# Two hybrid layers on one core: constant products in TensorE's first gaps, the large loads on one queue, eight tiles of key exponents, a new order

## The chip, the core and the metric

The kernel runs on one core of a Trainium2 chip. The core has five engines with an instruction queue each: TensorE (PE in the profile; its weight loads are PEld), VectorE (DVE), ScalarE (ACT), GpSimd (POOL) and SyncE (SP). TensorE writes its products to PSUM, eight banks here (`pb`), from which VectorE and ScalarE take them. Transfers are issued from the queues of SP and ScalarE and run on 16 DMA engines. The engines wait for one another by semaphores. The metric is device time in microseconds (us) of the core.

## The reference

For x of 2048 rows and 512 columns in bfloat16, the same two layers run twice:

```python
x = x + A(layernorm(x))     # linear attention, 32 heads of 16
x = x + B(layernorm(x))     # gated unit of width 1376
# A:
q, k, v = split(x @ wqkv)
phi(u)  = concat(softmax(u @ w_phi), softmax(-(u @ w_phi)))   # over 16
kv, z   = phi(k)^T v, sum over rows of phi(k)
o       = (phi(q) kv) / (phi(q) z + 1e-6)
A       = o @ wo
# B:
gate = x @ W_gate;  gate = gate * (gate > 0);  B = (gate * (x @ W_up)) @ W_down
```

The sums kv and z run over all 2048 rows, so no row can be attended before the keys of all rows are done.

## The kernel before

The 2048 rows are 16 tiles of 128, in five slabs of 2, 4, 4, 4 and 2 tiles (`SLABS`). All of x stays in SBUF (`x_sb`), as do the weights. At the start `fold` multiplies w_phi into the key and query weights: the weights are transposed (the key quarters on TensorE, the query quarters by transposing loads), multiplied with a block-diagonal matrix BD made of w_phi, and stored as `Wkp` and `Wqp`.

For each layer, `layernorm` takes statistics (L813, L838), a logarithm and an exponential for the standard deviation (L840, L842), applies them (L855 on ScalarE, L858 on VectorE or POOL), and turns the tile round, on TensorE or by a transposing load of SP's queue (L863). `keys` then makes, tile by tile, products with `Wkp` and `wv` (L682), two exponentials (L915, `expk`), their sums over 16 (L921, `Zk`), reciprocals (L924 on VectorE, L927 and L928 on ScalarE), a copy of the values (`vsb`), and the two value products with the reciprocals (L935, `vhat`, on VectorE or POOL). Of these, TensorE makes small products of 32 by 34 (L947) that are added up in `kvsum` (L957). `expk` and `vhat` have five buffers, used in turn. After the last tile `sums` builds the matrices of the sums; per slab `queries` makes the exponentials of the queries (L1016, `expq`), and `attend` the sums (L1031 or L1044), the softmax's divisor, its spreading to all rows (L1153 with products, or L1089 and L1093 by way of memory into `abT`), the numerators (L1105), their copies (`oT`, two buffers by slab), the product with `wo` and the residual. `glu` makes gate and up (L1227, L1229) and the product with W_down.

The order of the work is not that of the code. Each operation is recorded with a cost, and `Program.schedule` places them one after the other by start and by the turn numbers of the table `TURNS`; the table `ENG` names the engine of each movable operation. The order that comes out is fixed for every engine's queue: an engine that waits for one operation holds all behind it. TensorE's shape of array changes between plain products, small products, strips and numerators (`mode`).

Loads before: ScalarE issues x tiles 2 and 3, tile 0, and tiles 4 to 7; SP issues tile 1, a key quarter, w_phi, three key quarters, x tiles 8 to 11, wv, two transposing query loads, x tiles 12 to 15, and the rest.

The program's lines are these; the planner's function `schedule` and the build.

## Time and profile before

| what | before |
|---|---|
| time, median of 3 runs | 387.96 us (387.41 to 388.64) |
| profiled execution: time, span | 387.48 us, 385.7 us |
| TensorE busy | 370.9 us, 96% of the span |
| VectorE, ScalarE, POOL busy | 272.9, 200.6, 57.5 us |
| mean granted clock of TensorE | 0.991 |
| first key product starts | 12.90 us |
| VectorE ends layer 0's last value product | 57.6 us |
| first product of the gated unit | 76.89 us |
| TensorE's last product ends | 382.2 us |

The span runs from the first to the last instruction. A share of busy time is a mean over stages with different limits, so the stretches between the marks of the table are read one by one. A line such as `L1105 ... x32` is a group of 32 instructions of line 1105. A time after "idle" or "waited for" is time in which an engine had nothing it could do, with what ended it. Idle time costs only where the engine sets the pace. A matmul's duration holds its latency; products in a row start closer together than they last.

### The profile page before, as it was taken

Reading aid. Unit: us, or ns where it says so; the run is one execution under the profiler, and the core shown is the slowest. Engines: PE = TensorE matmul, PEld = TensorE weight load, DVE = VectorE, ACT = ScalarE, POOL = GpSimd, SP = SyncE. Lnnn points to the kernel's source line nnn. Section 1 sums busy time; section 2 is a strip of 40 time slices with the busy share of each in tenths; the row PEclk is TensorE's granted clock in tenths of the full one; section 3 lists DMA queues with packets and bytes.
Section 4 is the critical chain, followed back from the end, with each engine's and each line's share of the span. In section 5 each row is a group of like instructions: output and inputs, shape, how many; then the busy total and the mean of one; then the engine's idle time right before and its main releaser. Section 6 shows DMA issues by size and latency. Waiting matters only on the chain.

```text
span 385.7 us, 9001 instructions
## 1 busy us (share of the span) xinstructions
PE 370.9 (96%) x3713; PEld 197.6 (51%) x3767; DVE 272.9 (71%) x562; ACT 200.6 (52%) x447; POOL 57.5 (15%) x57
## 2 busy tenths in 40 slices
PE   5899998999999999999999999999999999999996
PEld 2544554484444444544466555475444454444574
DVE  6999998889554895574697897689954566453343
ACT  3899989853452524163246789983344224232111
POOL 2055550020310000000132461002002011000000
PEclk9799999999999999999999999999999999999999
DMA  8992301055351222021002010123524131221011
GB/s 245 271 347 38 66 3 51 14 160 88 111 97 44 57 41 56 10 59 29 0 9 56 3 30 4 58 61 110 131 62 135 45 86 36 59 43 41 2 34 55
DMA packets 56969, 27.44 MB, mean 71 GB/s; under 512 B 39168, under 2 KB 55264, under 8 KB 56928
## 3 DMA queue, kind: packets, MB, share of 16 engines
q1 hardware_dynamic: 55840, 25.88, 26.8%
q10 hardware_dynamic: 1088, 0.98, 0.8%
q8 instruction: 29, 0.48, 0.5%
q14 instruction: 12, 0.10, 0.1%
HBM read 14.73 MB, written 4.00 MB: 49 GB/s over the span
## 4 chain that ended last, share of the span: by engine, by line
PE 77%; ACT 10%; DVE 7%; issue 2%; DMA 2%; POOL 1%; ACTq 0%; DVEq 0%
PE pb L682 74%; ACT expq L1016 3%; DVE Zk L921 2%; DMA x_sb<-in_A_x_dram 2%; ACT expk L915 2%; DVE vhat L935 2%; POOL vhat L935 1%; PE pb L947 1%; PE pb L1105 1%; ACT vsb L789 1%; ACT ytile L855 1%; DVE expq L1171 1%; ACT oT L789 1%; ACT abT L789 1%; ACT yA L789 1%
## 5 line engine op out<-in xcount | busy, mean ns | idle before, releaser
L682 PE MATMUL pb<-Wd,hT 128*128 128x512 bf16 (+2 forms) x352 | 93.0, 372 | 0.8 <-issue 0.3
L682 PE MATMUL pb<-yG,Wu 128*128 128x512 bf16 (+1 forms) x396 | 93.3, 336 | 0.3 <-issue 0.2
L682 PE MATMUL pb<-yG,Wg 128*128 128x512 bf16 (+1 forms) x393 | 91.4, 336 | 0.4
L1227 ACT ACTIVATE gate_sb<-pb 128x512 bf16<-128x512 f32 x80 | 46.7, 596 | 75.8 <-PE pb L682 57.7
L1229 DVE TENSOR_TENSOR hT<-gate_sb,pb 128x512 bf16<-128x512 bf16 x80 | 53.4, 682 | 44.2 <-PE pb L682 25.2
L935 POOL TENSOR_TENSOR vhat<-vsb,rZk 128x544 bf16<-128x544 bf16 x38 | 41.1, 1103 | 133.5 <-DVE vhat L935 85.7
L1175 DVE TENSOR_TENSOR x_sb<-x_sb,pb 128x512 bf16<-128x512 bf16 x59 | 39.3, 681 | 30.4 <-PE pb L682 30.1
L682 PEld LDWEIGHTS pb<-yG,Wu 128*128 128x128 bf16 x400 | 38.9, 98 | 32.5 <-ACT gate_sb L1227 0.4
L682 PEld LDWEIGHTS pb<-yG,Wg 128*128 128x128 bf16 x400 | 38.7, 98 | 30.0 <-DVE hT L1229 0.5
L682 PEld LDWEIGHTS pb<-Wd,hT 128*128 128x128 bf16 (+1 forms) x363 | 35.1, 98 | 35.9 <-issue 1.0
L915 ACT ACTIVATE expk<-pb 128x512 bf16<-128x512 f32 x64 | 34.8, 616 | 17.0 <-PE pb L682 15.7
L813 DVE BATCH_NORM_STATS2 stats<-x_sb 128x6 f32<-128x512 bf16 x60 | 39.9, 682 | 2.8 <-DMA x_sb<-in_A_x_dram 2.4
L921 DVE TENSOR_REDUCE Zk<-expk 128x64 f32<-128x1024 bf16 x32 | 37.9, 1204 | 0.4 <-ACT expk L915 0.2
L682 PE MATMUL pb<-wv,yA 128*128 128x512 bf16 x123 | 37.1, 381 | 1.0 <-issue 0.5
L682 PE MATMUL pb<-Wkp,yA 128*128 128x512 bf16 x119 | 36.7, 385 | 0.9 <-issue 0.6
L1016 ACT ACTIVATE expq<-pb 128x512 bf16<-128x512 f32 x64 | 34.8, 638 | 1.5 <-PE pb L682 1.4
L682 PE MATMUL pb<-wo_sb,oT 128*128 128x512 bf16 x122 | 33.4, 379 | 0.4 <-ACT oT L789 0.2
L682 PE MATMUL pb<-yA,Wqp 128*128 128x512 bf16 (+1 forms) x148 | 31.3, 334 | 1.4 <-issue 1.0
L1138 POOL TENSOR_TENSOR expq<-expq,abT 128x1024 bf16<-128x1024 bf16 (+1 forms) x8 | 14.0, 1761 | 123.4 <-PE pb L682 58.6
L1195 ACT ACTIVATE gate_sb<-pb 128x192 bf16<-128x192 f32 x16 | 5.3, 333 | 47.2 <-PE pb L682 47.2
L855 ACT ACTIVATE ytile<-x_sb,nmr,rstd 128x512 bf16<-128x512 bf16 x31 | 24.4, 825 | 2.8 <-DVE nmr L847 2.7
L682 PEld LDWEIGHTS pb<-yA,Wqp 128*128 128x128 bf16 x160 | 14.3, 98 | 12.0 <-issue 1.0
(97 smaller groups left out, 337.4 us busy)
## 6 DMA issues: line engine op xcount, KB each, us to landing
abT<-spread SPq DMA_DIRECT2D x32, 128.0 KB
out_dram<-x_sb SPq DMA_DIRECT2D x15, 128.0 KB, 1.8
Wu<-in_B_W_up_dram SPq DMA_DIRECT2D x1, 1280.0 KB
Wg<-in_B_W_gate_dram SPq DMA_DIRECT2D x1, 1280.0 KB
Wd<-in_B_W_down_dram SPq DMA_DIRECT2D x1, 1280.0 KB, 14.9
sums_scr<-abT SPq DMA_DIRECT2D x5, 256.0 KB, 2.5
Zs<-sums_scr SPq DMA_DIRECT2D x5, 256.0 KB, 2.9
x_sb<-in_A_x_dram SPq DMA_DIRECT2D x2, 512.0 KB, 6.8
```

The source lines that it names most:

```text
L682: op("pe", lambda e: e.matmul(view(ps), lhsT, rhs, start=start, stop=stop), reads=reads, writes=[ps], occ=max(25.0, 0.4167 * n + 2.6), lat ...
L789: op("act", lambda e: e.activation(dst(), src(), ACT.Copy), reads=[ps] + reads, writes=writes, occ=115 + 0.714 * n, lat=240 + 0.714 * n, n ...
L813: op("dve", lambda e: e.bn_stats(stats[:, t, :], src()), reads=[res], writes=[R("st", t)], occ=580, lat=680, name=f"bn{t}")
L855: op("act", (lambda t, yb: lambda e: e.activation(ytile[:, yb, :], x_sb[:, t, :], ACT.Identity, bias=nmr[:, t, :], scale=rstd[:, t, :]))(t ...
L915: op("act", (lambda i, s, pk: lambda e: e.activation(expk[:, i, s, :], full(pk), ACT.Exp, scale=1.0 - 2.0 * s))(i, s, pk), reads=[pk], wri ...
L921: op("dve", (lambda i, zb: lambda e: e.tensor_reduce(Zk[:, zb, :], expk[:, i, :, :].rearrange("p s (h f) -> p (s h) f", f=16), AX.X, ALU.a ...
L935: op(eng, (lambda i, s, vb, rz: lambda e: e.tensor_tensor(vhat[:, i, s, :, :], vsb[:, vb, :, :], rZk[:, rz, s * 32:(s + 1) * 32].unsqueeze ...
L1016: op("act", (lambda c0, s, ps: lambda e: e.activation(eqv(st)[:, c0:c0 + per, s, :], ps.f32()[:, 0:per * n].rearrange("p (c n) -> p c n", ...
L1138: op(eng, lambda e: e.tensor_tensor(part, part, abT[:, c].rearrange("p (s n) -> p s n", s=2)[:, :, 0:n], ALU.mult), reads=Re + [R("abT", c ...
L1175: op("dve", lambda e: e.tensor_tensor(x_sb[:, t, :], x_sb[:, t, :], full(ps), ALU.add), reads=[R("x", t), ps], writes=[R("x", t)], occ=597 ...
L1227: op("act", (lambda gb, pg, k: lambda e: e.activation(gate_sb[:, gb, 0:k], pg.f32()[:, 0:k], ACT.Relu))(gb, pg, k), reads=[pg], writes=[R( ...
L1229: op("dve", (lambda gb, hb, pu, k: lambda e: e.tensor_tensor(hT[:, hb, 0:k], gate_sb[:, gb, 0:k], pu.f32()[:, 0:k], ALU.mult))(gb, hb, pu, k),
```

## The change

Four things change together.

First, `filler` adds 18 products of a constant matrix (128x256) into PSUM banks that nobody reads: eight with constants on both sides, and ten with the first quarter of `Wkp` as the moving side, so that they come after it. Of the ten, three stand in the order after slab 0's second norm.

Second, the loads: ScalarE's queue issues x tile 0 and two key quarters. SP's issues tile 1, w_phi, tiles 2 and 3, tiles 4 to 7, two key quarters, wv, tiles 8 to 11, the four transposing query loads, tiles 12 to 15, and then the rest. The planner's costs of loads change with it (delays, a bandwidth of 345 instead of 360, a limit on what a queue holds).

Third, `expk` and `vhat` have eight buffers instead of five. Three of the exponents lie in `abT`, three of the value tiles in `oT`, which are otherwise used in the attention. So that they are free for layer 1's keys, the attention of layer 0's slabs 3 and 4 is recorded ahead of layer 1's second slab.

Fourth, `TURNS` and `ENG` are new: the engines of many copies, applies and products change, among them BD from POOL to VectorE and three applies from VectorE or ScalarE to POOL. The last tile's down product is cut at column 384 instead of 256.

```diff
-LASTCUT = ((0, 256), (256, 512))
+LASTCUT=((0,384),(384,512)); FILL=(8,10); LOADLATE=(100,150)
...
-    DMA_BW = 360.0
+    DMA_BW = 345.0
+    RING = 5500.0
...
-                free[o.eng] = s + o.occ
+                free[o.eng] = max(s + o.occ, qfree - self.RING)
...
-        NY, NE, NV, NG, NH = 8, 5, 4, 3, 18
+        NY, NE, NOWN, NV, NG, NH = 8, 8, 5, 4, 3, 18
...
-        expk = sb("expk", [NE, 2, 512])
-        vhat = sb("vhat", [NE, 2, 32, 17])
+        expk_own = sb("expk", [NOWN, 2, 512])
+        vhat_own = sb("vhat", [NOWN, 2, 32, 17])
...
+        oT_flat = oT[:].rearrange("p g c n -> p (g c n)")
+
+        def expk(i):
+            return expk_own[:, i] if i < NOWN else abT[:, i - NOWN, :].rearrange("p (s n) -> p s n", s=2)
+
+        def vhat(i):
+            return vhat_own[:, i] if i < NOWN else oT_flat[:, 1088 * (i - NOWN):1088 * (i - NOWN) + 1088].rearrange("p (s h e) -> p s h e", s=2, e=17)
...
+        def filler(k, reads, src):
+            for i in range(FILL[k]):
+                ps = bank(f"fill{k}{i}")
+                op("pe", (lambda ps: lambda e: e.matmul(ps.f32()[:, 0:256], ones[:, 0:128], src, start=True, stop=True))(ps),
+                   reads=R_ones + reads, writes=[ps], occ=109, lat=275, name="fill")
+
+        filler(0, [], ones[:, 0:256])
...
+        def attended_to(L, st):
+            if (L, st) not in attended:
+                attended.add((L, st))
+                prog.tag = f"q{L}{st}"
+                queries(st, buf[st])
+                attend(L, st)
...
         fold("k", Wknat, Wkp)
+        filler(1, [R("W", "k", 0)], Wkp[:, 0, 0:256])
...
+                    if st == 1:
+                        attended_to(0, 3)
+                        attended_to(0, 4)
                     into_a(1, st)
```

## The prediction

> **What bounds the kernel now.** I read the page's busy shares first, then busy time by stretch, then the chain of work that ended last, then who waited for whom, and last TensorE's own timeline.

> ```profile
> PE 370.9 (96%) x3713; PEld 197.6 (51%) x3767; DVE 272.9 (71%) x562; ACT 200.6 (52%) x447; POOL 57.5 (15%) x57
> ```

> TensorE is busy for all but 14.8 of 385.7 us, so no change that leaves its products alone can win much more than what it idles, waits in small pieces, or runs slowly. Where that is, the windows tell (busy of PE, PEld, DVE, ACT, POOL; then clock, DMA share, GB/s):

> ```profile
> 0.00:8.88 8.88, 4.83 (x23) 2.28 (x24) 5.05 (x20) 3.49 (x6) 2.42 (x11) 0.96 0.78 232
> 8.88:57.60 48.72, 46.19 (x843) 25.03 (x851) 48.13 (x94) 45.09 (x106) 21.58 (x20) 0.94 0.57 150
> 57.60:76.90 19.30, 17.69 (x347) 8.99 (x354) 16.27 (x43) 17.33 (x43) 0.00 (x0) 1.00 0.12 32
> 76.90:211.00 134.10, 133.04 (x869) 70.37 (x881) 94.79 (x197) 55.13 (x116) 12.91 (x9) 1.00 0.26 59
> 211.00:272.00 61.00, 59.69 (x983) 34.17 (x1008) 49.77 (x98) 46.48 (x109) 15.10 (x13) 1.00 0.17 48
> ```

> From 8.88 to 57.60 (keys of layer 0) VectorE is busy for 48.13 of 48.72: it sets the pace. From 76.90 TensorE does. Between them (queries, first attention) TensorE and ScalarE are both some 90% busy. The chain agrees; these are pieces of it (start, length, what):

> ```profile
> 1.82 7.04 DMA x_sb<-in_A_x_dram
> ...
> 42.13 2.34 DVE Zk L921 x2
> ...
> 55.07 2.55 DVE vhat L935 x4
> ```

> The loads begin it; at 57.6 VectorE ends the last value tile of layer 0. Two waits lie in the start:

> ```profile
> POOL hT L777 <- DMA wphi<-in_A_w_phi_dram: 4.6, 1, 4.6
> ...
> DVE stats L813 <- DMA x_sb<-in_A_x_dram: 2.4, 1, 2.4
> ```

> And there the granted clock (the number before DMA share) is half:

> ```profile
> 4.86:8.17 3.31, 0.78 (x9) 0.43 (x8) 1.62 (x5) 1.58 (x4) 1.04 (x1) 1.00 1.02 303
> 8.17:15.00 6.83, 5.78 (x36) 3.80 (x38) 5.97 (x20) 4.82 (x12) 0.00 (x0) 0.50 1.23 291
> ```

> Last, what small product groups cost TensorE (start, length):

> ```profile
> 28.32 1.03 PE L682 MATMUL pb<-wv,yA 128*128 128x512 bf16 x4 [0.16 <-POOL vhat L935]
> 29.28 0.68 PE L947 MATMUL pb<-vhat,expk 128*32 128x34 bf16 x64
> 30.12 0.92 PE L682 MATMUL pb<-yA,Wqp 128*128 128x512 bf16 x4 [0.16 <-issue]
> ```

> **The change, part by part.** The sum is made against the profiled execution, 387.48 us, of which 385.7 is span; the median of the three runs is 0.48 above it.

> *Stage 1, to VectorE's last value tile (57.6).* VectorE's work there is 53.18 us (5.05 and 48.13). The new order lists give it two value copies more (0.60 start to start), three 128x512 copies yA<-pb more (0.33), and the block-diagonal product, which leaves POOL; they take away a copy of Wkp and one of Wqp (0.60 each), a reciprocal (0.46) and a value product (0.63). The trace has the block-diagonal product on POOL alone (1.04); on VectorE I bound it by 0.40 (128x512 tensor-scalar) and 0.74 (128x544 tensor-tensor), and take 0.65. Sum: 1.20+0.99+0.65-0.60-0.60-0.46-0.63 = +0.55, so 53.73. Its idle was 0.98 at the start, 0.39 in the constants, 2.40 for the x load and 0.59 after. The 2.40 should go: the four-tile x load moves from third of the ScalarE queue, behind 384 KB, to fourth of SP's, behind 400 KB, with 384 KB instead of SP's megabyte beside it; the 1.3 MB of both queues up to its end take 5.6 us at the first stretch's 232 GB/s, and the first microsecond moves next to nothing: about 6.6, against 8.88. But a new wait comes: the block-diagonal product now stands on VectorE ahead of the first applies, and waits for w_phi. That load goes from third to second of SP, 1.26 us instead of 1.72; landing took 5.0, so 6.3. VectorE gets there with 5.05 less two statistics (1.20) and an apply (0.32) done, at 4.9: a wait of 1.4 (0.4 if the queue ahead alone delays it, 1.9 if it lands as late as before). Everything behind it waits too: both first applies, and through them ScalarE's first apply and copies and TensorE's first keys. End of the stage: 0.98+0.39+1.4+0.59+53.73 = 57.1, **0.5 us sooner**. Bounds: 1.5 sooner (early w_phi); 0.8 later, if the last x load, now behind four transposing loads, lands late: issued near 12.5 instead of 9.3, at the 6.8 that such a load took it lands at 19.3, and VectorE wants it at 18.1 by its work; at 4 us (two less of queue) it is in time, and I take that, since the queue ahead is by then drained.

> ScalarE is no bound: its sum up to the first residual falls by 0.8 (four value and yA copies fewer net of the weight copies). TensorE's lead counts only where VectorE lets it: the last weight copy ends near 12 us instead of 13.75, and value products fill the wait for the third weight quarter.

> *The 18 constant products* are 128x256. Eight such in a row took 1.04 us at full clock, the last 0.27 of it alone, so 0.11 each: 1.96 us. Eight stand in the idle 5.0 to 8.2 and seven behind ScalarE's weight copies, covered by those waits; uncovered, each costs 0.11, at half clock 0.22. Three stand after the first transposes of slab 0's second norm, ahead of the gate products: 0.33, counted below. I take the clock at full from 8.2 on, worth nothing by itself while VectorE paces.
> The trace's clock fell at 8.2 after 3.31 us with 0.78 of products, the longest idle being 1.33. [...]

> *Eight tiles of exponents.* ScalarE waited 1.3 us for TensorE to free such a tile; that goes, hidden. More weighty, products of several tiles go together: layer 0 has five groups instead of nine. The three rows above price a group: a plain product is due 0.2157 after the one before, so at 29.18, and comes at 30.12: 0.94, of which the 64 small products need 0.52 (0.68 less 0.17 of latency). That leaves 0.42 for two changes of array shape; the attention's row groups cost 0.19 for two. By the order, changes fall from 86 to 67: 13 of them before the first gate product, 6 after.

> *Stage 2, 57.6 to 76.9.* At the last key group the old order has 16.1 us of products left to the first gate product, the new one 14.65 and 0.33 of fillers, with two changes of shape fewer (0.2). TensorE fills 17.69 of 19.30 here, so most of it counts: 1.3 less; I take **1.0**, since softmax of the sums, spreading and numerators are a chain of ScalarE and VectorE that stays (bounds 0 and 1.5).

> *From 76.9 on* the products are the same, 299.7 us. Six changes at 0.1 to 0.2: **0.5** (0 to 1.2). Slabs 3 and 4 attend earlier, so that layer 1's tiles 5 to 7 can use the spreading buffer and the oT buffer; the order has their keys 20 us of products after the last such reader, so no new wait. Their DMAs pass the second norm's transposes on SP; covered while TensorE is 99% busy (133.04 of 134.10). POOL gets three applies (128x512; not in the trace on POOL: 1.04 to 2.13 by its rows, 1.1 the nearest size); SP's transposes of those tiles wait for it, with sums and spreads behind. Covered likewise; uncovered, 1 to 2 us each.

> *The tail.* The last tile is cut 384/128: the last addition falls from 0.42 to 0.29 (128x128 rows), but waits for the larger one: **0.1** less.

> Sum: 0.5+1.0+0.5+0.1 = 2.1; 387.48-2.1 = 385.4, and with the median's 0.48 **385.8 us**.

> **The rivals.**
> *No lead.* w_phi or the last x load eats the first 0.5, the clock falls anyway and TensorE's share of stage 2 shrinks to 0.2: 0.5+0.1 later on remain: 387.1. For it: VectorE's work grew by 0.55, and nothing else of stage 1 is removed from it. [...]
> *Slower: POOL ends layer 1's values.* For layer 1 POOL now has 23 of 32 value products instead of 18, and the last 17 in a row; of tiles 10 to 15 it has 8 instead of 6. In the old trace it ended at 234.8 and the last key group began 2.9 later. Each product that ends later costs 1.08, since the attention of layer 1 starts from the sum of all of them and TensorE has by then run out of other products. Slower by 0.3% from three and a half products beyond the sum; with four, 390.1. Against it: eight tiles let keys run ahead, and POOL idled 4.6 of its last 18.9 us.
> *More.* The whole 1.5 of stage 1, 1.5 of stage 2 and 1.2 after: 383.6.

> **How the numbers follow.** 0.3% of 387.96 is 1.16 us, about what can be told from no change: faster is under 386.8, slower over 389.1. Forecast 0.47 (own range 384.4 to 387.0), more 0.16, no lead 0.19, slower 0.18. Faster: 0.42+0.16+0.08 = 0.66; same 0.05+0.11 = 0.16; slower 0.18. The range leaves out one in ten on each side: 383.2 to 389.6.

> **What would show it.** Right: VectorE's last value product of layer 0 near 57, the first gate product near 75.3, about 20 issue waits fewer before TensorE's groups, clock 1.00 from 8 to 15 us. Wrong: VectorE waiting at its first load of the last x tiles, POOL's last value product beyond 237, or TensorE waiting on VectorE or POOL for over 1 us between 211 and 245.

## The result: slower by 0.4%, and the profile after

The changed kernel takes 390.5 us (median) where the kernel before takes 388.3: a ratio of 1.0042, 95% interval 1.0026 to 1.0057, some 1.6 us slower (1.0 to 2.2) by all runs together. The forecast was 2.1 us faster, and its range ended at 389.6. The profiled execution took 390.13 us with a span of 388.4 (before: 387.48 and 385.7), so this pair lies 2.65 us apart, more than the ratio says; what follows divides up the pair.

The page's busy line after, and of its list of DMA queues the line on instructions (packets, MB, share):

```profile
PE 376.3 (97%) x3785; PEld 198.1 (51%) x3785; DVE 276.0 (71%) x563; ACT 191.9 (49%) x428; POOL 75.7 (19%) x68
...
q8 instruction: 30, 0.49, 0.6%
```

The windows after, same marks and columns as before (busy of PE, PEld, DVE, ACT, POOL; then clock, DMA share, GB/s):

```profile
0.00:8.88 8.88, 7.13 (x48) 3.93 (x48) 7.25 (x27) 5.48 (x12) 1.51 (x10) 1.00 0.75 227
8.88:57.60 48.72, 46.76 (x904) 24.60 (x902) 47.36 (x91) 43.88 (x105) 22.58 (x21) 1.00 0.58 151
...
76.90:211.00 134.10, 133.39 (x817) 69.54 (x814) 92.97 (x191) 51.92 (x111) 23.48 (x16) 1.00 0.24 54
211.00:272.00 61.00, 58.66 (x1026) 33.76 (x1026) 49.72 (x97) 41.69 (x97) 19.82 (x17) 1.00 0.17 47
```

The start went about as told: the clock is at full throughout, and the first gate product came at 75.8 instead of 76.9. The time was lost behind it. From the first gate product to the end of the last product, TensorE took 305.33 us before (76.89 to 382.22) and 309.23 after (75.79 to 385.02): 3.9 us more for the same 2,541 products. What TensorE waited for in that part (window 62 to 382 us; us in total, times, longest), the first two lines of the kernel before:

```profile
PE pb L682 <- issue: 1.6, 10, 0.2
PE pb L1153 <- ACT expq L1016: 0.4, 1, 0.4
```

The ten of 0.16 us are no waits: there products have no record, as is shown further down. The first three lines of the changed kernel:

```profile
PE pb L706 <- issue: 1.5, 1, 1.5
PE pb L706 <- DMA yG<-ytile: 1.5, 2, 0.8
PE pb L1062 <- issue: 0.6, 1, 0.6
```

Two kinds: 1.47 us for late transposes of SP, and 2.03 us in which nothing that the profile knows was awaited; together 3.5 of the 3.9. Where the larger of these stands is seen in TensorE's timeline (start, length, what; in brackets the idle time before):

```profile
221.50 0.94 PE L978 MATMUL pb<-vhat,expk 128*32 128x34 bf16 x96
222.28 1.01 PE L978 MATMUL pb<-oT,abT 128*32 128x34 bf16 x96
223.22 0.39 PE L706 MATMUL pb<-Wkp,yA 128*128 128x512 bf16 x1
223.45 0.38 PE L706 MATMUL pb<-wv,yA 128*128 128x512 bf16 x1
223.66 0.38 PE L706 MATMUL pb<-Wkp,yA 128*128 128x512 bf16 x1
225.51 0.38 PE L706 MATMUL pb<-wv,yA 128*128 128x512 bf16 x1 [1.47 <-issue]
```

The eight tiles put three groups of 64 small products in a row. In these rows a small product with its weight load is due every 8 ns (96 in 0.78 us), a plain one every 216 ns (223.45 to 223.66), so 384 instructions go by here in 1.7 us. The line `q8 instruction` gives 30 transfers of 16 KB for the some 7,600 instructions of TensorE's queue: by division one for about 255, and 256 by the places that follow. Counted by weight loads, products and separate waits, the two idle times stand at places 192 and 193 of a block of 256, and each of the 30 places 193, 449 and so on has one transfer near it (from 3.2 us before TensorE passes it to 3.7 after):

| boundary passed | next block's transfer | next boundary reached | and passed |
|---|---|---|---|
| 222.02 us | 223.19 to 224.12 | about 223.9 | 225.51 (1.39 after the transfer) |
| 238.88 us | 240.05 to 241.03 | about 241.8 | 242.34 (1.31 after) |

So the theory to test, an inference from these two rows, was: *a boundary can't be passed before the transfer that the last one set off has landed and 1.3 us have gone by, some 3 to 4 us in all*. By it, 128 products that take longer than that cost nothing, and the two stalls here 2 us. The kernel before met it once, at 214.38 us (passed 1.31 us after its transfer; the weight load there came 0.4 late, its product 0.2).

### The profile page after: what moved, and what is told of

The parts are those of the page before. It is cut to its first block, busy times and chain, and to the rows that moved or that the text cites. A ratio compares the mean times of both kernels' runs of the same rounds, so it can differ in the third digit from the quotient of the medians.

```text
span 388.4 us, 9066 instructions
## 1 busy us (share of the span) xinstructions
PE 376.3 (97%) x3785; PEld 198.1 (51%) x3785; DVE 276.0 (71%) x563; ACT 191.9 (49%) x428; POOL 75.7 (19%) x68
## 4 chain that ended last, share of the span: by engine, by line
PE 83%; DVE 11%; DMA 4%; issue 1%; ACT 0%; DVEq 0%
PE pb L706 78%; DVE stats L844 3%; DMA yG<-ytile 2%; PE pb L978 2%; DVE Zk L952 2%; DVE expq L1202 1%; DMA yA<-ytile 1%; PE pb L1136 1%; DMA x_sb<-in_A_x_dram 1%; PE pb L1075 1%; DVE yA L817 1%; DVE ytile L889 1%; PE pb L1062 1%; DVE vsb L817 0%; DVE mv L869 0%
## 5 line engine op out<-in xcount | busy, mean ns | idle before, releaser
L706 PE MATMUL pb<-yG,Wg 128*128 128x512 bf16 (+1 forms) x400 | 97.1, 337 | 0.0
L706 PE MATMUL pb<-Wd,hT 128*128 128x512 bf16 (+4 forms) x363 | 95.4, 373 | 0.0
L706 PE MATMUL pb<-yG,Wu 128*128 128x512 bf16 (+1 forms) x400 | 91.8, 336 | 0.0
L966 POOL TENSOR_TENSOR vhat<-vsb,rZk 128x544 bf16<-128x544 bf16 x31 | 33.5, 1101 | 55.7 <-DVE rZk L955 18.6
L1169 POOL TENSOR_TENSOR expq<-expq,abT 128x1024 bf16<-128x1024 bf16 (+1 forms) x11 | 20.7, 1899 | 118.1 <-DMA abT<-spread 61.6
L706 PE MATMUL pb<-yA,Wqp 128*128 128x512 bf16 (+1 forms) x160 | 34.5, 338 | 0.9 <-DVE Zk L952 0.7
L946 ACT ACTIVATE expk<-pb 128x512 bf16<-128x512 f32 x40 | 21.9, 612 | 10.0 <-PE pb L706 8.8
L952 DVE TENSOR_REDUCE Zk<-expk 128x64 f32<-128x1024 bf16 x20 | 24.2, 1209 | 1.4 <-ACT expk L946 1.2
L886 ACT ACTIVATE ytile<-x_sb,nmr,rstd 128x512 bf16<-128x512 bf16 x27 | 20.9, 807 | 0.5 <-DVE nmr L878 0.4
L706 PEld LDWEIGHTS pb<-Wkp,yA 128*128 128x128 bf16 x128 | 12.2, 98 | 15.9 <-issue 1.8
```

The lines of the kernel that those rows point to most:

```text
L706: op("pe", lambda e: e.matmul(view(ps), lhsT, rhs, start=start, stop=stop), reads=reads, writes=[ps], occ=max(25.0, 0.4167 * n + 2.6), lat ...
L886: op("act", (lambda t, yb: lambda e: e.activation(ytile[:, yb, :], x_sb[:, t, :], ACT.Identity, bias=nmr[:, t, :], scale=rstd[:, t, :]))(t ...
L946: op("act", (lambda i, s, pk: lambda e: e.activation(expk(i)[:, s, :], full(pk), ACT.Exp, scale=1.0 - 2.0 * s))(i, s, pk), reads=[pk], wri ...
L952: op("dve", (lambda i, zb: lambda e: e.tensor_reduce(Zk[:, zb, :], expk(i).rearrange("p s (h f) -> p (s h) f", f=16), AX.X, ALU.add))(i, z ...
L966: op(eng, (lambda i, s, vb, rz: lambda e: e.tensor_tensor(vhat(i)[:, s], vsb[:, vb, :, :], rZk[:, rz, s * 32:(s + 1) * 32].unsqueeze(2).to ...
L1169: op(eng, lambda e: e.tensor_tensor(part, part, abT[:, c].rearrange("p (s n) -> p s n", s=2)[:, :, 0:n], ALU.mult), reads=Re + [R("abT", c ...
```

## Experiments

They go by ratios to the kernel before, run on the same chip each time; one of 0.001 is 0.39 us. The rival theory was that the late transposes and the new turns are the loss, and the idle times put down to issue belong to what stands there.

**Shifting every place.** The edit replaces warming products at the start by small ones, so that all later instructions of TensorE stand a number of places further on; no other instruction, order or wait changes (here 232; `(2, 21)` gives 80, and in the kernel before `(1, 13)` gives 24).

```diff
+SHIFT = (4, 30)
...
+        def warmed(i):
+            def fn(e):
+                if i >= SHIFT[0]:
+                    return e.matmul(full(warm), ones[:, 0:128], ones[:, 0:512], start=True, stop=True)
+                for j in range(SHIFT[1]):
+                    q = 32 * (j % 4)
+                    ins = e.matmul(warm.f32()[q:q + 32, 0:34], ones[:, 0:32], ones[:, 0:34], start=True, stop=True, skip_group_check=True, tile_position=(0, q))
+                return ins
+            return fn
...
-            op("pe", lambda e: e.matmul(full(warm), ones[:, 0:128], ones[:, 0:512], start=True, stop=True),
-               reads=R_ones, writes=[warm], occ=427, lat=640, name="warm")
+            op("pe", warmed(i), reads=R_ones, writes=[warm], occ=427, lat=640, name="warm")
```

> The changed kernel with 116 more products at its start (the first four warming products of 128x512 become 120 small ones of 32x34, ahead of all work), so that every later instruction of TensorE stands 232 places further on in its queue; order, waits and all other engines are as in the changed kernel. Theory 'blocks': the queue takes its instructions in blocks of 256 (the trace's transfers named instruction, 16 KB each); by the weight loads' start times the boundaries lie at places 193+256n, and the next boundary can't be passed sooner than about 3.45 us after the last (222.0 to 225.5 and 238.9 to 242.3 us in the trace). With 232 places more no two boundaries lie closer than that after 62 us, so the idle times of 1.47 and 0.56 us put down to issue vanish and the kernel is about 1.9 us shorter than the changed kernel: 388.6, level with the kernel before at 388.3. Rival 'transposes and turns': those two stalls are of something at that place of the work (a queue, a port), the loss comes from late transposes and the new turns; then the stalls stay and the time is 390.5 within 0.5.

Measured: 388.24 us, ratio 0.9985 (0.9964 to 1.0006): 0.0057 below the changed kernel, 2.2 us. TensorE's waits of 62 to 382 us, the two longest:

```profile
PE pb L707 <- DMA yG<-ytile: 0.7, 1, 0.7
PE pb L1146 <- DVE expq L1212: 0.5, 1, 0.5
```

No line on issue is left. The same work in the same order on every engine, and 2 us less: the theory of blocks holds and the rival falls for the two stalls. The 2.2 us aren't the stalls alone, though: of the two waits for transposes one is gone too (0.67 us are left of 1.47).

> The same edit with 40 more products at the start (the first two warming products become 42 small ones): 80 places. Theory 'blocks': by the same rule stalls of 2.3 us near 226 and 2.3 us near 244 (two boundaries within the small products of each), with 1.2 near 59 and 1.9 near 34, where part is covered by VectorE's pace: 2.7 us slower than the changed kernel if only the two late ones count (393.2), 3.9 with the one at 59 (394.4), 5.9 at most. Rival 'transposes and turns': 390.5 within 0.5.

Measured: 392.41 us, ratio 1.0091 (1.0056 to 1.0126), 0.0049 above the changed kernel: 1.9 us (six runs), with an uncertainty of about 1.5. The median is below the 2.7 told, the sign and the places are right; both late stalls now stand inside groups of small products, and a third of 1.00 us stands in one at 57.8 us (TensorE's timeline):

```profile
224.20 0.43 PE L988 MATMUL pb<-oT,abT 128*32 128x34 bf16 x36 [1.92 <-issue]
...
241.98 0.22 PE L988 MATMUL pb<-oT,abT 128*32 128x34 bf16 x7 [2.45 <-issue]
```

The two are 2.3 us longer than before the shift, but from the first gate product to the last product TensorE takes only 0.7 longer (table below): in that stretch it never waits for a late transpose here. A stall gives late tiles time to come, so the two kinds of wait don't simply add up.

> The kernel before with 12 more products at its start (its first warming product becomes 13 small ones): 24 places. Theory 'blocks': the kernel before has no stall of this kind over 0.35 us only because of where its boundaries fall; 24 places on, they give 1.9 us near 213, 0.8 near 242 and 0.35 near 60: 2.7 us slower, 391.0, as slow as the changed kernel. Rival 'transposes and turns': 388.3 within 0.5.

Measured: 391.13 us, ratio 1.0055 (1.0028 to 1.0083), 2.1 us slower, where 2.7 was told. The size fits, but the cause isn't shown. The profiled execution was the quickest of its runs (389.2; they go up to 394.96) and shows no stall at 213: there the transfer left at 210.45, ahead of its boundary at 212.23. From the first gate product to the last product it takes 305.41 us, as much as the kernel before; the 1.7 us that it is longer lie ahead of that, where VectorE waited 1.1 and 0.6 us for ScalarE. That the slower runs lost their time in stalls, because the transfer left later in them, is a guess, since none of them has a trace.

**Splitting instead of shifting.** The third of the three groups moves behind nineteen plain products; all places ahead of it stay.

```diff
+MOVED = [(("kv2", 2), ("v13", 6), True)]
...
         prog.schedule()
+        named = {}
+        for o in prog.ops:
+            named.setdefault(o.name, []).append(o)
+        for (name, k), (other, j), after in MOVED:
+            named[name][k].start = named[other][j].start + (0.01 if after else -0.01)
         prog.plan()
```

> The changed kernel, with its own places, and one group of 64 small products (the third of three groups that follow one another at 221.5 to 223.2 us) moved behind 16 to 18 plain products. Theory 'blocks': from the boundary at 222.0 to the next there are then some 64 small and 16 to 18 plain products before the rest, more than the 3.45 us that a block takes; the stall of 1.47 goes, two more changes of array shape cost 0.2 to 0.4: 1.1 to 1.3 us shorter than the changed kernel, 389.3, ratio to before 1.001. The stall of 0.56 at 242 stays. Rival 'place': the stall belongs to the products behind it (a tile or a load that they wait for): it stays at 225.5 or moves with them, 390.5 to 390.9.

Measured: 389.89 us, ratio 1.0016 (0.9995 to 1.0036): 1.0 us below the changed kernel, as told, with an uncertainty of about 1. In the timeline the products that waited for 1.47 us no longer do, and the group follows later without a stall; a stall of 1.0 at 243.4 stays:

```profile
223.68 0.45 PE L979 MATMUL pb<-oT,abT 128*32 128x34 bf16 x32
224.05 0.39 PE L707 MATMUL pb<-Wkp,yA 128*128 128x512 bf16 x1
...
227.41 0.81 PE L707 MATMUL pb<-wv,yA 128*128 128x512 bf16 x3
228.15 0.66 PE L979 MATMUL pb<-oT,abT 128*32 128x34 bf16 x64
```

**The constant products and the clock.** First the changed kernel with products of 16 columns.

```diff
-                op("pe", (lambda ps: lambda e: e.matmul(ps.f32()[:, 0:256], ones[:, 0:128], src, start=True, stop=True))(ps),
+                op("pe", (lambda ps: lambda e: e.matmul(ps.f32()[:, 0:16], ones[:, 0:128], src[:, 0:16], start=True, stop=True))(ps),
```

> The changed kernel with each of the 18 constant products cut from 256 columns to 16, so that their number, place and waits stay and only their work goes. Theory of the prediction (the clock from 8 to 15 us is worth nothing, since VectorE paces, and the three late ones cost 0.33 on the path): 0.2 to 0.4 us shorter, 390.2. Rival 'the products earn their keep': the granted clock falls to one half from about 8 us as in the kernel before, and TensorE, which in the changed kernel has next to no idle time up to 37 us, then sets the pace there: 1 to 3 us longer, 391.5 to 393.5.

Measured: 390.58 us, ratio 1.0034 (1.0010 to 1.0059), 0.3 us below the changed kernel, with an uncertainty of 1.1: the rival's loss of 1 us and more doesn't show, and 0.33 for the three late products can't be told from nothing. In the profiled execution the clock didn't fall. Windows of it:

```profile
4.86:8.17 3.31, 2.02 (x32) 1.61 (x29) 2.60 (x8) 2.86 (x8) 0.00 (x0) 1.00 1.00 328
8.17:15.00 6.83, 6.45 (x111) 3.51 (x108) 6.83 (x22) 6.22 (x14) 0.00 (x0) 1.00 1.11 274
```

With 2.02 us of products in the first window, against 0.78 in the kernel before, the full clock stays without the constants' work. They make it surer: the mean granted clock was 0.991 to 0.996 in four of this run's 12 executions, and 0.995 at the lowest in the changed kernel's 34. (Where half of the warming products were gone too, in a224 below, that window had 0.69 and the clock fell for 3.4 us; in a224u, which starts alike, it had 1.47 and the clock held.) Then the kernel before with its places shifted by 112, alone and with sixteen constants between the transposes of the key weights:

```diff
                     tr(ps, (lambda kc: lambda p: p.b16()[:, kc * 128:(kc + 1) * 128])(kc), Wnat[:, ic, kc * 128:(kc + 1) * 128], [R_Wnat[w][ic]], f"wtr{w}")
+                    if w == "k":
+                        extra(prog.ops[-1], ps, 2 if kc % 2 else 0)
...
+                for _ in range(n):
+                    e.matmul(ps.f32()[:, 256:512], ones[:, 0:128], ones[:, 0:256], start=True, stop=True, skip_group_check=True)
```

> The kernel before with 56 small products ahead of its eight warming products (112 places). Theory 'blocks': no boundary of this kernel comes sooner than 3.45 us after the last, so it loses the 0.33 us at 214 that the rule gives for the kernel before, and is level with it or up to 0.5 shorter: ratio 0.998 to 1.000. A ratio over 1.003 would speak against the rule that was read from the weight loads' times.

> The kernel before with 40 small products ahead and 16 constant products of 128x256 placed two by two between the transposes of the key weights, in the unused half of the same PSUM bank: also 112 places, and the new kernel's constant products without its loads, buffers and order. Prediction: the clock is worth nothing by itself there, since VectorE paces; the same time as b112 within 0.5, whether the granted clock at 8 to 15 us is 1.00 or 0.50. Rival: the full clock pays, 0.5 to 1 us shorter than b112; or the products stand in the way of the weights, 0.5 to 1.5 longer.

Measured: 388.84 us, ratio 0.9993 (0.9976 to 1.0010), and 388.46 us, ratio 0.9983 (0.9960 to 1.0005). The windows differ in the clock above all (the first is of the shifted kernel, the second of the one with constants):

```profile
8.17:15.00 6.83, 5.92 (x36) 3.42 (x35) 6.37 (x21) 5.22 (x12) 0.13 (x1) 0.52 1.32 263
```

```profile
8.17:15.00 6.83, 5.71 (x53) 3.69 (x54) 5.72 (x18) 4.66 (x12) 0.35 (x1) 1.00 1.42 277
```

The difference, 0.4 us with an uncertainty of 1.1, is no evidence of a gain; from these two runs alone a full microsecond isn't excluded. More is seen in the kernel before, unchanged. Its 116 executions that went beside these runs each have a mean granted clock: 0.99 in 73 of them, as in the profiled one with its 6.8 us at half clock, and 0.995 or more in 43. Taken chip by chip, the 43 are 0.36 us shorter, with an uncertainty of 0.41. So the full clock is worth less than a microsecond there, if anything.

**The late transposes.** On a232, three places of the order were changed in the same way.

```diff
+MOVED = [(("apply4", 1), ("nmr2", 1), True), (("zai3", 0), ("ytx4", 0), True), (("zao3", 1), ("ytx2", 2), True)]
```

> a232 with three places changed in the written order: the fourth tile of slab 1's second norm (layer 0) is applied on VectorE right after the three small products before it instead of two steps later; SP reads the sums of slab 3 back only after all four transposes of that norm instead of between them; in layer 1 it writes the sums of slab 3 out after two of the transposes of slab 1's second norm instead of ahead of them. Theory 'transposes': TensorE's one wait of 0.7 us for a transposed tile at 91 us (0.71 and 0.76 in the changed kernel) goes, and TensorE is busy behind it, so 0.7 shorter than a232: some 387.5 where before has 388.3 to 389.5, a ratio to before of 0.9967. Rival 'next wait': the products that come earlier meet the next late work (exponents of queries at 64 to 67 us don't move; the spread of slab 3 comes 0.2 later): no gain, ratio 0.9985.

Measured: 389.75 us, ratio 1.0002 (0.9973 to 1.0032), no gain. It was a bad experiment, for two reasons. First, the apply that was moved forward now met a product of POOL. VectorE's row, and POOL's:

```profile
81.75 2.12 DVE L900 TENSOR_SCALAR ytile<-x_sb,mv,rstd 128x512 bf16<-128x512 bf16 x1
```

```profile
79.51 4.21 POOL L1180 TENSOR_TENSOR expq<-expq,abT 128x1024 bf16<-128x1024 bf16 x2 [0.29 <-DMA abT<-spread]
```

The apply took 0.41 us elsewhere and 2.12 here, to the end of POOL's second product. Second, the wait at 91 us did go, but TensorE had others: 0.72 us on issue at 241.9, where it passed a boundary 1.34 us after the transfer, and 0.71 for a transposed tile at 279.7. a232 had passed the same boundary 1.30 us after its transfer without a stall that shows, so its places leave no room there. Before SP alone was moved, the best shift was looked for, with the constants at 16 columns and 224 places (`SHIFT = (4, 29)`), beside the changed kernel again, a run that tells VectorE's pace from TensorE's (`kvs` 1 behind `Zk11` 0 by the same means), and one that both splits and shifts (240 places).

> The changed kernel again, unchanged, beside the three below. Theory 'blocks': its two stalls stand at the same places of the order (in front of the plain product at 225.5 us and inside the row groups at 242.3), 3.3 to 4.0 us after the boundary before each, whatever else differs; together 2.0 to 2.8 us. If they were chance, they would be elsewhere or gone. Ratio to before 1.0042 within 0.002.

> The changed kernel with its 18 constant products cut to 16 columns and 112 more products at the start (four warming products become 116 small ones): 224 places. Theory 'blocks': at this place the boundaries leave 0.7 us near 52, where VectorE's work covers part, and nothing after; the three late constant products cost 0.3 less. So 2.0 to 2.5 us shorter than the changed kernel: ratio to before 0.997 to 0.999. Rival 'a floor': TensorE gives back what it gains at the next late transposes, as with the moved transposes; ratio 1.000 or more.

> a224 with one addition of key sums on VectorE (the one that waited 0.59 us at 43.7 for a group of 128 small products of TensorE) moved behind the next reciprocal and the next sum over 16. If VectorE paces layer 0's keys to the end, as the prediction has it, the matrices of the sums begin 0.6 us sooner (58.46 in the changed kernel) and the first gate product too. If the large groups have made TensorE the one that paces from 37 us on, as the chain of the changed kernel shows it, the addition is no longer in the way but its end hardly moves: 0 to 0.2 sooner.

> The changed kernel with the group of 64 small products moved as in the split run, its constant products cut to 16 columns and 240 places. Theory 'blocks': of the split run's one stall of 1.0 near 243, 0.5 to 1.0 is left and none elsewhere; with the late constant products 0.3 less: 0.3 to 0.8 us shorter than the split run, ratio to before 0.9995 to 1.001. It tells whether splitting and shifting reach the same time (a224) or the two extra changes of shape keep it above.

Measured: the changed kernel again 390.21 us, ratio 1.0031 (1.0009 to 1.0053), its two stalls at the same two places (1.5 and 0.8); a224 388.53 us, 0.9990 (0.9968 to 1.0012); a224k 388.84 us, 0.9994 (0.9969 to 1.0020); as240 389.56 us, 1.0015 (0.9992 to 1.0039), a miss by its median though not by its interval: a stall of 0.5 was left, as told, and TensorE waited 0.9 for VectorE. In a224k the matrices of the sums began at 59.16, in a224 at 58.91: one wait of 0.5 for TensorE was gone, and waits of 0.4 and 0.3 for ScalarE had come. Moving the addition won nothing, which fits that VectorE no longer sets the pace there (one execution each, and in a224's the clock fell near 8 us, in a224k's not).

The second profile of the same program settles a reading. Its busy line and TensorE's waits of 62 to 383 us:

```profile
PE 371.7 (96%) x3736; PEld 198.2 (51%) x3785; DVE 275.2 (71%) x563; ACT 191.9 (49%) x428; POOL 75.7 (19%) x68
```

```profile
PE pb L706 <- issue: 2.4, 7, 1.5
```

Here 49 products have no record, and six more "issue" waits appear, for the same instructions. So the 0.16 us rows of this kind before TensorE's groups are products that weren't recorded. The weight loads have no such gaps: in the kernel before, behind the group of small products that the prediction priced, five loads stand where its row shows four products:

```profile
29.28 0.56 PEld L947 LDWEIGHTS pb<-vhat,expk 128*32 128x32 bf16 x64 [0.42 <-DVE yA L786]
29.89 0.76 PEld L682 LDWEIGHTS pb<-yA,Wqp 128*128 128x128 bf16 x5
```

At last SP's two moves on a224, without the apply:

```diff
+MOVED = [(("zai3", 0), ("ytx4", 0), True), (("zao3", 1), ("ytx2", 2), True)]
```

> a224 with SP's order alone changed at the two places (the sums of slab 3 read back after all four transposes of slab 1's second norm in layer 0, and written out after two of them in layer 1), without the earlier apply that met GpSimd's product. SP then issues the third transpose 0.6 us sooner and the fourth at once when its tile is applied (86.6 instead of 87.7). Theory 'transposes': the wait of 1.05 us at 91.4 falls to 0.3 or less and the time by 0.5 to 1.0 against a224: ratio to before 0.9965 to 0.998. Rival 'next wait': the wait goes, but the first products of the gated unit that follow meet another late tile, and the time stays: 0.999.

Measured: 387.81 us, ratio 0.9984 (0.9963 to 1.0004), against 0.9990: too small a step to be told by times. TensorE's longest waits from 77 us on, first of a224, then of a224u (the rows on issue left out are products without a record, 0.2 at most):

```profile
PE pb L707 <- DMA yG<-ytile: 1.1, 1, 1.1
...
PE pb L707 <- ACT abT L956: 0.5, 1, 0.5
```

```profile
...
PE pb L708 <- DVE x_sb L1217: 0.5, 1, 0.5
PE pb L708 <- DMA yA<-ytile: 0.3, 1, 0.3
```

The wait of 1.05 for transposes is gone, and one of 0.47 for an addition of VectorE at 94.1 stands instead. In the table below a224u's stretch is 0.64 us shorter, but one kernel's repeats differ by up to 0.9 there, so neither theory is decided.

The stretch from the first gate product to the end of the last product sums it up (one execution each; the repeats of the changed kernel and the shifted versions of the kernel before show how much it varies):

| kernel (its profiled execution) | first gate product | end of last product | between |
|---|---|---|---|
| before | 76.89 | 382.22 | 305.33 |
| before, 24 places | 78.55 | 383.96 | 305.41 |
| before, 112 places | 77.73 | 383.62 | 305.89 |
| changed | 75.79 | 385.02 | 309.23 |
| changed, again | 75.18 | 385.27 | 310.09 |
| changed, 80 places | 75.98 | 385.89 | 309.91 |
| changed, one group split off | 76.88 | 385.85 | 308.97 |
| changed, 232 places | 76.21 | 383.18 | 306.97 |
| changed, 224 places, small constants | 76.24 | 383.27 | 307.03 |
| the same, SP's two moves (a224u) | 75.81 | 382.20 | 306.39 |

a224u is clearly below the changed kernel (1.0042 and 1.0031), and its times lie under those of the kernel before by 0.16%, with an interval that takes in no difference. No version beat the kernel before beyond doubt.

## Why the prediction was wrong, point by point

**Stage 1: 0.5 sooner.** Right by its mark, partly by luck, and then given back. VectorE ended its last value product of layer 0 at 56.9 (before: 57.6; told: 57.1). The wait of 1.4 for w_phi didn't come in this execution, and the last x tiles were in time; in its place VectorE worked 54.27 us up to the mark where 53.73 was told, and had new waits of 0.59 and 0.29. The block-diagonal product took 0.66, as told. But the additions of the key sums now wait for TensorE's groups of small products (VectorE's timeline, start and length):

```profile
43.70 0.44 DVE L988 TENSOR_TENSOR kvsum<-kvsum,pb 128x272 f32<-128x272 f32 x1 [0.59 <-PE pb L978]
...
57.99 0.44 DVE L988 TENSOR_TENSOR kvsum<-kvsum,pb 128x272 f32<-128x272 f32 x1 [0.71 <-PE pb L978]
```

The last of these waits was 0.19 before, so 0.5 of the 0.7 was lost, and the matrices of the sums began 0.16 sooner. The first of them waits for a group of 128. Grouping saves TensorE changes of shape (about 0.2 us for two, by the weight loads at 29 us) and lets whoever needs the group wait for all of it (the 0.59 and 0.71 above); the working had only the first.

**What sets the pace.** "The chain agrees" isn't so for the first part: in the kernel before, 21.8 of the chain's 28.1 us from 8.88 to 37 are ScalarE's, and VectorE has 17.8 of the 20.6 from there to 57.6. In the changed kernel VectorE has 23.6 of the first part, and TensorE 18.2 of the second. So "VectorE paces" came to hold up to 37 us only, and "ScalarE is no bound" was read from its sum of work alone.

**Stage 2: 1.0.** From the matrices of the sums on, 0.9 (58.46 to 75.79, against 58.62 to 76.89), about right; from the prediction's own mark, VectorE's last value product, only 0.4, since the 0.5 just named lies between. The lead at the first gate product was 1.1, where 1.5 was told.

**The constants.** Clock as told (full from 8 us, no gain that can be measured). Their 0.33 is too small for the times to show. In the run with 16 columns the clock held in most executions without their work.

**Eight tiles; a group priced at 0.42; 20 issue waits fewer.** The price was read from rows with a missing product. By the weight loads the plain load stands 0.14 behind the last small one, not 0.37, so two changes of shape cost about 0.2. The sum behind stage 1 used 0.1 to 0.2 a change and stands. The sign "20 issue waits fewer" came true and said nothing: the changed kernel's profile happens to hold all 3785 products.

**From 76.9 on, "the products are the same": 0.5 sooner.** This is the step that failed. TensorE needed 3.9 us more instead. The working priced small products by their own duration and by their changes of shape, and TensorE's supply of instructions at nothing. Of the 4.4 us between, 2.03 are the two stalls and 1.47 the two waits for transposes of the next point. Shifting alone took the stalls away, and with them some waiting for transposes (2.2 us by the first pair of ratios, 1.6 by a224, with its smaller constants, beside the second run of the changed kernel, each with an uncertainty of about 1). The planner in the kernel knows the blocks (`CHUNK`, `FETCH`) but counts two instructions for a product and none for a separate wait, of which TensorE's queue has 47 before 222 us: its boundaries lie that far off. That this is why it made such an order is argued, not shown.

**Transposes "covered while TensorE is 99% busy".** Also wrong: 0.71 and 0.76 us of TensorE's waits are for transposes of a second norm, at 90.85 and 278.5. At the first, SP's reading back of slab 3's sums (attention moved ahead) stands between them. Between a224 and a224u, where such a wait of 1.05 was removed, the stretch got 0.64 shorter, which is within what repeats differ by. The rest of the loss, about 1 us between a224u and the kernel before, stays open: a224u's trace has waits of 0.2 to 0.5 for VectorE and SP there, but which of them cost time wasn't tested.

**POOL.** An apply took 2.07 us, at the upper end of the bounds and not the 1.1 taken; nobody waited for it. The rival "POOL ends layer 1's values" gave 390.1, near the time measured, by a mechanism that didn't happen: POOL's last value product ended at 236.3, before the 237 from which it was to decide, and TensorE never waited for it. By its own price of 1.08 three late products, not three and a half, would have passed its mark of 389.1.

**The tail: 0.1.** From the last product's end to the end of the span 3.48 us before, 3.38 after: right.

## What to carry to other kernels

Before small products are put together in long rows, count instructions: here, where 128 products with their loads took less than the 3.0 to 4.0 us that a block took in these traces, TensorE came to wait 0.4 to 2.45 us for something that the profile calls "issue" without a cause; that it waits for its own program is inferred. Whether such a loss came depended on where the blocks of 256 fell (2.03 us in the changed kernel, none 232 places on), so a version that lost or won some 0.5% after any edit should be run once more with the places shifted before the edit is judged. And before a small idle time is given a price, compare the counts of products and weight loads: a missing record looks like a wait (49 products without one in the second profile of the changed kernel, and six waits more).
